# Four layers on one core: the order of every engine replaced, and each PSUM copy and residual given an engine of its own

## The chip, the cores and the metric

One Trainium2 chip, of which the program uses one core. The metric is the device time of one execution in microseconds. Of the kernel before there are three runs: 394.34, 394.36 and 395.02 us, median 394.36.

## The reference

x has 2048 rows of 512 bf16 numbers. Four layers follow one another, A, B, A, B, each `x = x + layer(layernorm(x))`, with 32 heads of 16:

```python
def _A_ref(x, wqkv, w_phi, wo):            # linear attention
    q, k, v = heads(x @ wqkv)
    pq, pk = q @ w_phi, k @ w_phi          # per head
    phi_q = concat([softmax(pq), softmax(-pq)])
    phi_k = concat([softmax(pk), softmax(-pk)])
    kv = phi_k^T @ v;  z = sum over rows of phi_k
    return (phi_q @ kv) / (phi_q @ z + 1e-6) @ wo

def _B_ref(x, wqkv, wo):                   # each row looks at rows s, s-2, ..., s-14
    q, k, v = heads(x @ wqkv)
    attn = softmax(q . k[s - 2*w] * 0.25)  # w = 0..7
    return sum_w attn * v[s - 2*w] @ wo
```

kv and z of a layer A are sums over all 2048 rows, so nothing of that layer's second half can begin before its last row has been through the first half.

## The kernel before

The rows are cut into four blocks of 512, each of four tiles of 128. L counts the two A-B pairs (0 and 1), b the blocks (0 to 3); "10" below is L = 1, b = 0. The work of a block is a chain of stages:

- `s_ln_first` and `s_norm` (L303 to L391): sums and squares of a tile (VectorE L371, ScalarE L382), variance (L309 to L313), reciprocal root on ScalarE (L317, L320), normalised tile (VectorE L325), transposes on TensorE (L338), copies of the transposed halves out of PSUM (L344): one half on ScalarE, one on VectorE.
- `s_fold` (L219) multiplies the query and key weights of layer A with w_phi once: transposes (L229), copy wT (L233), product (L238), copy WA (L242). `s_load_B` loads the weights of B and reorders them on GpSimd (L263). `s_bound` squares WA on GpSimd (L285) for a test of the range.
- `s_a1`: key and value products (L451, L463), exponentials Ek (ScalarE L457), value copies vaug (ScalarE L470), softmax sums and product (VectorE L477 to L497), then kv for all blocks in three PSUM banks (L506). `s_a2`: query products (L534), exponentials Eq (L540). `s_akv`: kv out of PSUM (VectorE L575, L582); this is the barrier of the layer, "akv0" and "akv1" below.
- `s_a3`: denominators (L603 to L622) and the product with Eq (L635, or L655 where the factor went through DRAM). `s_a4`: numerator (L680), copy oT (ScalarE L686), and in `s_out` the output product (L401), the residual (VectorE L414), squares for the next norm (ScalarE L421), and `s_norm` again.
- `s_b1`: q, k and v of layer B (L702), each copied out of PSUM by ScalarE (L716). `vrep` (L745) copies V of a block 16 times shifted within SBUF, from SP's queue: 16 DMAs of 131 KB, tiles Vg. `s_b2`: products of Q with eight shifts of K (VectorE L770), summed on TensorE (L777), exponential, softmax. `s_b3`: products with Vg (VectorE L830, "pav"), summed on TensorE (L837), copy oT (L843), then `s_out`; in the last layer `s_out` stores.

Every operation is a step, filed under a stage and an engine. `_ORDER` (L45) is a list of base-36 numbers, one for each step: it says which stage and engine gets its next step recorded. So it fixes the order on TensorE, VectorE, ScalarE and SP, each of which takes its list strictly in turn and waits by semaphore, and also the order in which buffers are handed out: 8 PSUM banks, 8 big SBUF buffers (Ek, prod, Vg, pav), 16 medium ones.

Of the kernel before, what the change touches and what calls it, by code (L numbers as in the profile page):

```python
# [8 lines left out]
BF16 = mybir.dt.bfloat16  # L9
# [7 lines left out]
P = 128  # L17
NJ = 16
D = 512
# [17 lines left out]
_OPT = {"rho_dma": ((0, 2), (0, 3), (1, 2), (1, 3)), "pe_resid": {}, "tr_dma": (), "stat_act": (), "fold_act": 0,  # L37
        "evac_act": ()}
# [7 lines left out]
1 1 0 1 0 1 i 0 i 0 i i 0 1 i 0 i 0 2 i 0 2 0 2 1 2 c 0 m n d m 3 4 m n 3 4 m 3 n 3 c n f e c g 4 c d c 4 c f  # L46
3 e 6 e 6 4 7 6 7 3 3 5 a 9 5 a 9 a 9 a 9 4 3 9 5 7 3 t u 6 d j j 5 r j 3 a 7 j 9 9 h j 9 r 9 j s 6 j s 7 j r
s 6 j r s 6 6 j s 6 k j s s j k l l k l l k l b l b b l b 8 l 9 8 8 s 8 o t a t v 7 15 u o u 15 v 16 o 16 15 6
16 o 15 16 v 16 y 16 16 y 16 z y 19 z z y 19 z 17 18 17 z 17 z z 17 z p t 12 18 10 11 o 10 u 10 11 18 v 10 12
11 w q 19 q 11 19 q v 18 q f f f h f h 12 1a x g x 12 x 19 x g 1g 13 12 1k 1g 1h 1h 1g 1h 1h 1g 1h 1h 14 1h 14  # L50
1k 14 1h 1g 14 1h 1e 1e 1f 1f 1e 1f 1f 1e 1f 1f 1b 1f 1b 1b 1f 1e 1b 1f 1n 1c 1n 1n 1n 1n 1c 1d 1n 1d 1c 1d 1d
1c 1d 1d 2c 1d 1i 1d 2d 1o 2e 1j 1c 2d 1j 2c 1d 1i 2d 1p 2c 1j 2d 1q 2d 1i 1j 1p 1i 2d 1j 1j 2d 1o 1j 2d 1j 1p
1i 1p 3r 1j 1p 1o 1p 1p 31 1p 1l 1p 1l 1p 1m 1r 1r 1m 1s 1r 1s 32 1r 1s 2d 1s 1t 2d 33 1t 1u 32 1t 1v 1u 34 1t
1u 1v 3s 2f 1v 2f 1u 2g 2f 2g 2f 34 1v 1u 34 2g 1v 2g 2h 1u 3t 1u 1t 1u 1t 2i 2h 1v 1u 1t 3s 2j 1t 2i 2h 3u 1u
2j 2h 34 2i 1y 1z 2i 1y 32 3u 2j 3u 1y 2j 2i 1y 1z 2j 1w 1z 2i 1z 2i 2h 2i 1x 2h 2i 1w 2j 2q 32 2h 2h 1x 35 2i
35 36 23 35 36 3u 35 36 2o 36 2o 23 2o 2o 3s 1w 1w 1x 3s 2k 1x 23 2k 2l 2k 2l 2k 2l 23 3v 2l 3v 3w 3v 3w 3v 3w
2m 3w 2m 2n 2s 2m 2n 2m 2n 20 21 2s 2t 2n 20 20 21 2s 2t 21 20 37 2s 21 22 21 2t 2p 22 37 2p 22 2p 22 38 37 2p
22 38 39 22 2t 38 2r 2u 37 2r 2u 3g 2r 2t 38 39 2r 3x 2u 2r 2r 3x 3y 2r 39 2s 3x 2r 39 38 2r 3x 2p 2r 3z 3y 2r
39 24 3y 2r 3z 24 2r 38 3z 24 38 2r 38 37 2r 38 37 37 2r 3y 39 37 24 22 38 22 3z 2v 22 3e 3f 22 3e 22 22 25 3e
22 3f 2v 22 25 2w 22 3f 3e 22 2x 3a 3f 2v 3f 3h 2w 3b 3h 3a 2x 3h 3h 3a 3b 2v 3h 3h 2w 3b 3h 3a 2x 3h 3h 3c 3y  # L60
3b 23 3h 3z 2w 3h 3d 3y 24 3h 3y 2x 3y 2y 3h 25 3y 3h 3i 2y 3h 3h 2y 2y 2z 3j 2z 30 3x 3x 2z 30 3x 3x 3c 2z 3z
3y 3c 30 23 30 40 2z 3d 26 40 30 41 40 3d 41 40 41 26 42 41 42 43 26 42 43 42 43 27 43 26 27 28 27 28 44 45 3i
44 28 27 45 44 28 3i 29 45 29 29 2a 29 2a 2b 2a 3j 2b 3j 2a 2b 44 2z 2b 2a 2y 45 2z 3c 2z 2b 47 2z 2y 3d 47 2a
2y 2y 2a 30 47 29 2a 29 47 2a 29 2b 3i 47 4q 4r 47 29 47 4q 47 47 4o 4r 2a 47 2z 47 3j 4p 47 46 59 3k 48 47 3k
47 4q 4p 47 5a 4q 47 5a 48 3j 4r 59 4r 3k 59 48 59 5a 5a 4o 5a 5a 4o 3i 4p 4o 4p 4p 49 4p 49 4p 48 4p 49 5a 4h
5a 59 4i 3l 4i 49 5a 4h 4a 4h 4a 3l 4i 3m 4i 49 3n 4h 4a 3l 3m 5b 3n 4i 5b 5c 48 5c 3m 3l 5c 5b 3n 5c 5b 5c 5c
4j 4k 4b 3m 4j 5c 3n 4b 3o 5c 4i 4c 4i 3o 4d 4i 4b 3o 4k 4c 3o 4d 4b 4c 5b 4d 4j 5c 3p 4c 4k 3p 4j 3q 3p 4d 4e
3q 3p 3q 4e 4f 3q 3p 4e 4g 4f 3q 4e 4f 4k 4g 3p 3p 4g 3o 3p 3o 3p 3q 3o 4f 3o 3p 4g 4v 4f 4s 4v 4g 4w 4v 4w 4f
4f 4w 4v 4f 4w 4f 4w 4s 4x 4y 4l 4x 4w 4s 4x 4l 4y 4w 4s 4x 4y 4l 4t 4e 4e 4e 4y 4e 4l 5d 4f 4w 4g 4s 5d 5e 5d
# [12 lines left out]
7w 7v 7b 7w 7b 7x 7b 6p 7w 7b 7x 7b 7w 7x 7b 7b 6q 7x 82 7b 6q 6r 7b 6q 6r 7y 7z 82 83 7y 6r 7y 7z 82 83 7z 7y
7z 82 83 81 81 81 81 7f 81 83 81 84 81 84 83 81 81 7f 7g 84 81 81 81 7h 81 81 82 7g 81 7f 81 7h 7f 7g 7h 6p 7g
7h 7i 85 6q 7i 6r 85 86 6s 85 87 86 6s 87 85 6s 86 6s 87 7j 7i 7j 86 7j 7k 7i 87 6t 6t 88 7j 6u 88 6t 7k 88 6t
89 6u 88 89 89 8a 89 8a
"""


class _Fast:

    def __init__(self, ctx, tc, A_x, A_wqkv, A_w_phi, A_wo, B_wqkv, B_wo, out):
# [14 lines left out]
        for n in ("xnT", "oT", "Eq", "rS", "kvp", "K", "QT", "Vg", "PT", "vh"):  # L106
            setattr(self, n, {})
# [18 lines left out]
    def step(self, stage, eng, fn, *args):  # L126
        key = stage + "." + eng
        if key not in self.threads:
            self.threads[key] = []
            self.names.append(key)  # L130
        self.threads[key].append(lambda: fn(*args))

# [84 lines left out]
    def s_fold(self, qk):  # L217
# [14 lines left out]
        def ev(pr, copy):  # L232
            copy(out=T["wT"][:, pr * 2:pr * 2 + 2, :].rearrange("p a b -> p (a b)"), in_=T[pr][:])  # L233

# [6 lines left out]
        def ev2(m, copy):  # L241
            copy(out=self.WA[:, m, qk * D:(qk + 1) * D], in_=T["f", m][:])  # L242

        for pr in range(2):
            add(st, "PE", tr, pr)
            add(st, *(("DVE", ev, pr, nc.vector.tensor_copy) if pr == 0 and not _OPT["fold_act"] else
                      ("ACT", ev, pr, nc.scalar.copy)))
        for m in range(NB):
            add(st, "PE", mm, m)
            add(st, *(("DVE", ev2, m, nc.vector.tensor_copy) if m % 2 == 0 and not _OPT["fold_act"] else  # L250
                      ("ACT", ev2, m, nc.scalar.copy)))
# [52 lines left out]
    def s_norm(self, st, key, b, T):  # L304
        nc, add = self.nc, self.step

        def var():
            T["q"] = self.sm([4], "q")
            nc.vector.scalar_tensor_tensor(out=T["q"][:], in0=T["sums"][:], scalar=-1.0 / D, in1=T["sums"][:],  # L309
                                           op0=ALU.mult, op1=ALU.mult)  # L310
            T["nm"] = self.sm([4], "nmean")
            nc.vector.tensor_scalar(out=T["nm"][:], in0=T["sums"][:], scalar1=-1.0 / D, scalar2=None, op0=ALU.mult)
            nc.vector.tensor_tensor(out=T["q"][:], in0=T["q"][:], in1=T["ss"][:], op=ALU.add)  # L313

        def ln():
            T["lnv"] = self.sm([4], "lnv")
            nc.scalar.activation(out=T["lnv"][:], in_=T["q"][:], func=ACT.Ln, bias=self.eps_t[:, 0:1],  # L317
                                 scale=1.0 / D)
            T["rstd"] = self.sm([4], "rstd")
            nc.scalar.activation(out=T["rstd"][:], in_=T["lnv"][:], func=ACT.Exp, scale=-0.5)  # L320

        def ap(t):
            if t == 0:
                T["xn"] = self.med([4, D], "xn")
            nc.vector.tensor_scalar(out=T["xn"][:, t, :], in0=self.x[b][:, t, :], scalar1=T["nm"][:, t:t + 1],  # L325
                                    scalar2=T["rstd"][:, t:t + 1], op0=ALU.add, op1=ALU.mult)
# [1208 lines left out]
```

## Time and profile before

| | |
|---|---|
| runs, median | 394.36 us |
| profiled execution | 393.82 us, its span 392.1 us |
| TensorE busy | 341.3 us, 87% of the span |
| VectorE busy | 321.6 us, 82% |
| ScalarE busy | 273.8 us, 70% |
| GpSimd busy | 19.9 us, 5% |
| mean granted TensorE clock | 0.965 |

The span runs from the first to the last instruction; the execution's own time is 1.72 us longer. PE is TensorE, DVE VectorE, ACT ScalarE, POOL GpSimd, SP the engine that issues most DMAs. A row of the timeline has start and length in us, engine, line, operation, tiles; in brackets the idle time before it and who ended it. A row of a group has busy us, mean ns of one, and idle before it. A row of a stretch has, for each engine, its busy time and instructions, then the granted clock, the DMA share and GB/s.

### The profile page before, as it was taken

To read this page: it belongs to the slowest core of one execution; us is meant where nothing else is said; L and a number is where in the kernel's file an instruction comes from. 1 tells how busy PE (TensorE), PEld (TensorE's weight loads), DVE (VectorE), ACT (ScalarE), POOL (GpSimd) and SP (SyncE) were. 2 spreads that over 40 slices of the span, in tenths; PEclk is the share of its full clock that TensorE was granted. 3 is DMA by queue.
4 is the path that set the end of the run, shared out by engine and by line. 5 is a ranking of instruction groups with operands and counts; after the bars stand their busy time and mean duration, and the time that the engine had idled before them with its cause. 6 is when DMAs were issued, how large, how long until landed. Compare 5 with 4: busy or idle time off the path is not lost.

```text
span 392.1 us, 7308 instructions
## 1 busy us (share of the span) xinstructions
PE 341.3 (87%) x2841; PEld 159.0 (41%) x2841; DVE 321.6 (82%) x484; ACT 273.8 (70%) x619; POOL 19.9 (5%) x40
## 2 busy tenths in 40 slices
PE   1859998989999997999999999969999978993691
PEld 1525465543444332444433457533443322331130
DVE  6684594288798886999899988599799868997993
ACT  5779986867757885768997998656977773663220
POOL 2250007200000000000000000000000000000000
PEclk9959999999999999999999999999999999997598
DMA  8920000001520599954800000044000399698404
GB/s 248 351 48 0 2 0 2 2 3 32 143 56 0 108 152 151 163 93 94 128 3 0 3 0 3 5 112 115 2 1 2 76 151 160 146 165 160 80 29 142
DMA packets 17242, 30.65 MB, mean 78 GB/s; under 512 B 4272, under 2 KB 11952, under 8 KB 17200
## 3 DMA queue, kind: packets, MB, share of 16 engines
q1 hardware_dynamic: 16672, 30.09, 38.7%
q8 instruction: 24, 0.39, 0.5%
q14 instruction: 18, 0.15, 0.1%
q10 hardware_dynamic: 528, 0.02, 0.1%
HBM read 10.50 MB, written 2.36 MB: 33 GB/s over the span
## 4 chain that ended last, share of the span: by engine, by line
PE 52%; DVE 18%; ACT 12%; DMA 10%; SPq 3%; issue 2%; POOL 0%; ACTq 0%; DVEq 0%; POOLq 0%
PE ps L702 16%; DMA Vg<-V 10%; PE ps L451 7%; PE ps L401 6%; PE ps L463 6%; PE ps L534 4%; SPq L745 3%; DVE x L414 3%; PE ps L338 3%; DVE pav L830 3%; DVE Eq L635 3%; PE ps L777 3%; PE ps L506 2%; ACT sqd L421 2%; DVE Ek L497 2%
## 5 line engine op out<-in xcount | busy, mean ns | idle before, releaser
L702 PE MATMUL ps<-xnT,WB 128*128 128x512 bf16 x384 | 89.8, 379 | 1.0 <-DVE xnT L344 0.8
L830 DVE TENSOR_TENSOR pav<-PT,Vg 128x4096 bf16<-128x4096 bf16 x32 | 71.9, 2288 | 9.5 <-DMA Vg<-V 9.4
L770 DVE TENSOR_TENSOR prod<-QT,K 128x4096 bf16<-128x4096 bf16 x32 | 71.8, 2285 | 3.8 <-ACT K L716 1.9
L702 PEld LDWEIGHTS <-WB 128*128 128x128 bf16 x384 | 35.4, 98 | 49.5 <-issue 10.5
L414 DVE SCALAR_TENSOR_TENSOR x<-ps,x 128x512 bf16<-128x512 f32 x64 | 41.1, 686 | 2.0 <-PE ps L401 1.6
L401 PEld LDWEIGHTS <-oT 128*128 128x128 bf16 x256 | 23.5, 98 | 35.6 <-issue 7.1
L540 ACT ACTIVATE Eq<-ps 128x512 bf16<-128x512 f32 x64 | 33.6, 615 | 4.9 <-PE ps L534 4.9
L421 ACT ACTIVATE sqd<-x 128x512 bf16<-128x512 bf16 x48 | 29.9, 625 | 7.9 <-DVE x L414 7.8
L843 ACT CAST oT<-ps 128x512 bf16<-128x512 f32 x32 | 18.7, 590 | 22.5 <-PE ps L837 22.5
L457 ACT ACTIVATE Ek<-ps 128x512 bf16<-128x512 f32 x64 | 33.5, 670 | 0.3 <-PE ps L451 0.3
L837 PE MATMUL ps<-pav,indAV 128*32 128x512 bf16 x256 | 20.9, 417 | 14.0 <-DVE pav L830 14.0
L338 PE MATMUL ps<-ident,xn 128*128 128x128 bf16 x256 | 20.8, 231 | 14.0 <-DVE xn L325 11.3
L401 PE MATMUL ps<-WoA,oT 128*128 128x512 bf16 x128 | 30.8, 380 | 1.4 <-ACT oT L686 1.1
L534 PE MATMUL ps<-xnT,WA 128*128 128x512 bf16 x128 | 30.1, 379 | 2.1 <-DVE WA L242 1.6
L463 PE MATMUL ps<-WA,xnT 128*128 128x512 bf16 x128 | 31.8, 397 | 0.1
L401 PE MATMUL ps<-WoB,oT 128*128 128x512 bf16 x128 | 31.2, 388 | 0.1
L451 PE MATMUL ps<-WA,xnT 128*128 128x512 bf16 x128 | 30.4, 391 | 0.5 <-ACT xnT L344 0.5
L716 ACT CAST V<-ps 128x512 bf16<-128x512 f32 x32 | 18.5, 588 | 14.9 <-PE ps L702 14.7
L325 DVE TENSOR_SCALAR xn<-x,nmean,rstd 128x512 bf16<-128x512 bf16 x64 | 23.4, 424 | 4.9 <-ACT rstd L320 4.9
L338 PEld LDWEIGHTS <-xn 128*128 128x128 bf16 x256 | 16.8, 103 | 21.8 <-DVE xn L325 16.6
L716 ACT CAST QT<-ps 128x512 bf16<-128x512 f32 x32 | 18.8, 590 | 9.4 <-PE ps L702 9.2
L716 ACT CAST K<-ps 128x512 bf16<-128x512 f32 x32 | 18.5, 585 | 9.6 <-PE ps L702 9.5
(109 smaller groups left out, 449.9 us busy)
## 6 DMA issues: line engine op xcount, KB each, us to landing
Vg<-V SPq DMA_DIRECT2D x128, 131.5 KB, 5.8
Prho<-rd SPq DMA_DIRECT2D x8, 512.0 KB, 4.7
out_dram<-x SPq DMA_DIRECT2D x8, 256.0 KB, 2.2
x<-in_A_x_dram SPq DMA_DIRECT2D x3, 512.0 KB, 8.1
wbraw<-in_B_wqkv_dram SPq DMA_DIRECT2D x3, 512.0 KB, 8.8
wraw<-in_A_wqkv_dram SPq DMA_DIRECT2D x2, 512.0 KB, 6.2
x<-in_A_x_dram SPq DMA_DIRECT2D x4, 128.0 KB, 2.4
WA<-in_A_wqkv_dram SPq DMA_DIRECT2D x1, 512.0 KB, 4.0
```

Of the source, the lines that this page charges most:

```text
L338: nc.tensor.transpose(T["pt", t // 2][:, (t % 2 * NB + c) * P:(t % 2 * NB + c + 1) * P], T["xn"][:, t, c * P:(c + 1) * P], self.ident[:])
L401: nc.tensor.matmul(y[:], lhsT=oT[:, c, t * P:(t + 1) * P], rhs=Wo()[:, c, :], start=(c == 0), stop=(c == NB - 1 and t not in pe_res))
L414: nc.vector.scalar_tensor_tensor(out=xb[:, t, :], in0=T[t][:], scalar=1.0, in1=xb[:, t, :], op0=ALU.mult, op1=ALU.add, **kw)
L421: nc.scalar.activation(out=sqd[:], in_=xb[:, t, :], func=ACT.Square, accum_out=T["ss"][:, t:t + 1])
L451: nc.tensor.matmul(pk[:], lhsT=xnT[:, t, k, :], rhs=self.WA[:, k, D:2 * D], start=(k == 0), stop=(k == NB - 1))
L463: nc.tensor.matmul(pv[:], lhsT=xnT[:, t, k, :], rhs=self.WA[:, k, 2 * D:3 * D], start=(k == 0), stop=(k == NB - 1))
L534: nc.tensor.matmul(pq[:], lhsT=self.WA[:, k, hb * P:(hb + 1) * P], rhs=xnT[:, :, k, :], start=(k == 0), stop=(k == NB - 1))
L540: nc.scalar.activation(out=self.Eq[L, b][s][:, :, hb, :], in_=T[hb][:].rearrange("p (t i) -> p t i", t=4), func=ACT.Exp, scale=1.0 - 2.0 * s)
L702: nc.tensor.matmul(pp[:], lhsT=self.WB[:, k, i, c, :], rhs=xnT[:, :, k, :], start=(k == 0), stop=(k == NB - 1))
L716: nc.scalar.copy(out=dst, in_=T[i, c][:])
L770: nc.vector.tensor_tensor(out=pr[:], in0=QT[:, c:c + 1, :].to_broadcast([P, NW, TB]), in1=win, op=ALU.mult)
L830: nc.vector.tensor_tensor(out=pv[:], in0=PT[:].unsqueeze(1).to_broadcast([P, NB, 2, TB]), in1=vw, op=ALU.mult)
```

## The change

Four things change.

1. `_ORDER` is replaced as a whole: 1423 steps instead of 1515 (the four vrep steps of a quarter are one step now).
2. Each copy out of PSUM, and each residual, is a step of its own kind (`flex`), and a string `_CHOICE` of 0 and 1 tells its engine. For a copy 1 means VectorE, 0 ScalarE. For a residual 0 means VectorE as before; 1 means that TensorE adds x with an identity matmul into the same PSUM bank and ScalarE writes the sum back. 27 of 64 residuals are so: 8 of the first A-B pair and 19 of the second.
3. The first layer norm uses BN_STATS and BN_AGGR on VectorE, without squares on ScalarE, and block 0 is normalised in two halves, tiles 2 and 3 first.
4. Memsets of a ones column, and of the first halos of K and V, become GpSimd steps that the order places.

The diff, cut to its core (two lines of the table stand for it):

```diff
-_OPT = {"rho_dma": ((0, 2), (0, 3), (1, 2), (1, 3)), "pe_resid": {}, "tr_dma": (), "stat_act": (), "fold_act": 0,
-        "evac_act": ()}
+_OPT = {"rho_dma": ((0, 2), (0, 3), (1, 2), (1, 3)), "tr_dma": ()}
...
-1 1 0 1 0 1 i 0 i 0 i i 0 1 i 0 i 0 2 i 0 2 0 2 1 2 c 0 m n d m 3 4 m n 3 4 m 3 n 3 c n f e c g 4 c d c 4 c f
...
+4 1r 4 0 5 4 0 1 4 4 6 6 0 0 2 0 2 3 n o n 7 16 16 p n q n r n n t 15 8 8 8 8 16 16 1a u u s 13 8 19 9 8 8 8 8
...
+    def flex(self, stage, fn, *args):
+        k = self.nflex
+        self.nflex += 1
+        self.step(stage, "F%d%s" % (k, fn.__name__), fn, *args, _CHOICE[k] == "1")
+
+    def copy(self, dve, out, in_):
+        if dve:
+            self.nc.vector.tensor_copy(out=out, in_=in_)
+        else:
+            self.nc.scalar.copy(out=out, in_=in_)
...
+            def stat(t):
...
+                nc.vector.bn_stats(out=T["stat"][:, t - t0, :], in_=self.x[b][:, t, :])
+                nc.vector.bn_aggr(out=T["mv"][:, t - t0, :], in_=T["stat"][:, t - t0, :])
...
+        if b == 0:
+            part((0, 1))
+            part((2, 3))
+        else:
+            part((0, 1, 2, 3))
...
+        def mm(t, onpe):
...
+            if onpe:
+                nc.tensor.matmul(y[:], lhsT=self.ident[:], rhs=xb[:, t, :], start=False, stop=True)
...
+        def res(t, onpe):
...
+            if onpe:
+                kw = {} if last else {"accum_out": T["sums"][:, t:t + 1]}
+                nc.scalar.activation(out=xb[:, t, :], in_=T[t][:], func=ACT.Identity, **kw)
...
-            add(st, "ACT", ev, t)
+            self.flex(st + "v", ev, t)
...
-        for dl in range(4):
-            for g in range(4):
-                add(st + "v", "SP", vrep, dl, g)
+        for dl in range(4):
+            add(st + "v", "SP", vrep, dl)
```

Three places in the order. The first is VectorE's start, from the mask product PHI on (x_84 is block 0 of x, x_85 block 1). Before:

```order
L212 TENSOR_TENSOR PHI<-phis,maskH 128x512
L371 TENSOR_REDUCE sums<-x_84 128x1 x4
L309 SCALAR_TENSOR_TENSOR q<-sums 128x4
L312 TENSOR_SCALAR nmean<-sums 128x4
L313 TENSOR_TENSOR q<-q,ss 128x4
L325 TENSOR_SCALAR xn<-x_84,nmean,rstd 128x512 x4
L344 COPY xnT<-ps 128x1024
L233 COPY wT<-ps 128x1024
L371 TENSOR_REDUCE sums<-x_85 128x1 x4
L233 COPY wT<-ps 128x1024
L242 CAST WA<-ps 128x512
L309 SCALAR_TENSOR_TENSOR q<-sums 128x4
```

After, from the second pair of statistics on:

```order
L379 BN_STATS stat<-x_84 128x6
L380 BN_AGGR mv<-stat 128x2
L379 BN_STATS stat<-x_84 128x6
L380 BN_AGGR mv<-stat 128x2
L384 COPY q<-mv 128x2
L379 BN_STATS stat<-x_84 128x6
L380 BN_AGGR mv<-stat 128x2
L334 TENSOR_SCALAR xn<-x_84,q,rstd 128x512 x2
L384 COPY q<-mv 128x2
L334 TENSOR_SCALAR xn<-x_84,q,rstd 128x512 x2
L146 COPY xnT<-ps 128x1024
L146 COPY wT<-ps 128x1024
```

Block 0 is normalised in two pairs of tiles; after its copies come block 1's four statistics, with one copy of the folded weights ahead of them and none behind them (the rest is ScalarE's).

The second is ScalarE in the second half of layer pair 1, where block 0's projected V leaves PSUM. Before (the last V row is block 0's fourth cast):

```order
L344 COPY xnT<-ps 128x1024
L716 CAST V<-ps 128x512 x2
L716 CAST K<-ps 128x512 x4
L317 ACTIVATE lnv<-q,eps_t 128x4
L320 ACTIVATE rstd<-lnv 128x4
L716 CAST QT<-ps 128x512
L784 ACTIVATE E,stE<-ps 128x512 x2
L716 CAST QT<-ps 128x512 x3
L716 CAST V<-ps 128x512
L798 ACTIVATE lnd<-ps,tiny_t 128x512
L800 ACTIVATE rden,stR<-lnd 128x512
L716 CAST V<-ps 128x512
```

After (L148 is the helper for copies on ScalarE; the last two V casts and the two before them are block 0's, in the order third, fourth, first, second):

```order
L148 CAST QT<-ps 128x512
L148 CAST K<-ps 128x512 x2
L148 CAST QT<-ps 128x512
L148 CAST V<-ps 128x512
L148 CAST oT<-ps 128x512 x2
L148 CAST V<-ps 128x512
L148 CAST K<-ps 128x512
L148 CAST oT<-ps 128x512
L148 COPY xnT<-ps 128x1024 x2
L148 CAST K<-ps 128x512
L148 CAST V<-ps 128x512 x2
```

Before, block 1's K and Q stand between block 0's V casts; now block 0's V is mostly among its own Q and K, with one K of block 1 ahead of the last two casts. On TensorE the fourth V projection of block 0 is the eleventh projection after the barrier now; it was the twentieth, with the output products and transposes of three other blocks among them. Its first two V casts stand on ScalarE behind block 1's transposed halves (xnT) and first K cast.

The third is VectorE's end. Before:

```order
L830 TENSOR_TENSOR pav<-PT,Vg 128x4096 x7
L414 SCALAR_TENSOR_TENSOR x_86<-ps,x_86 128x512 x3
L414 SCALAR_TENSOR_TENSOR x_85<-ps,x_85 128x512 x2
L414 SCALAR_TENSOR_TENSOR x_86<-ps,x_86 128x512
L414 SCALAR_TENSOR_TENSOR x_85<-ps,x_85 128x512 x2
L414 SCALAR_TENSOR_TENSOR x_87<-ps,x_87 128x512 x4
L864 TENSOR_REDUCE tot<-ps 128x1
```

After:

```order
L843 TENSOR_TENSOR PT<-E,rden 128x1024
L868 TENSOR_TENSOR pav<-PT,Vg 128x4096 x6
L421 SCALAR_TENSOR_TENSOR x_84<-ps,x_84 128x512
L421 SCALAR_TENSOR_TENSOR x_86<-ps,x_86 128x512
L421 SCALAR_TENSOR_TENSOR x_84<-ps,x_84 128x512
L421 SCALAR_TENSOR_TENSOR x_86<-ps,x_86 128x512 x3
L902 TENSOR_REDUCE tot<-ps 128x1
```

Twelve residuals behind the last product have become six; those of blocks 1 and 3 and half of block 0's are ScalarE's. The last products are block 2's and no longer block 3's.

308 lines of the change are left out of this document (158 added, 150 removed).

## The prediction

> **What bounds the kernel now.** I read the page's totals and clock row first, then the busy time of each engine by stage, then the timeline of the first 28 us, the chain of waits over the end, and the groups by line for durations.
>
> ```profile
> span 392.1 us, 7308 instructions
> PE 341.3 (87%) x2841; PEld 159.0 (41%) x2841; DVE 321.6 (82%) x484; ACT 273.8 (70%) x619; POOL 19.9 (5%) x40
> PEclk9959999999999999999999999999999999997598
> core 0: us, PE busy (x) PEld busy (x) DVE busy (x) ACT busy (x) POOL busy (x), PEclk, DMA share, GB/s
> 0.00:27.00 27.00, 13.04 (x97) 8.41 (x98) 20.46 (x53) 17.43 (x44) 9.56 (x30) 0.86 0.77 235
> 8.00:27.00 19.00, 13.04 (x97) 8.41 (x98) 14.77 (x31) 13.08 (x33) 7.15 (x16) 0.81 0.78 239
> 27.00:73.00 46.00, 43.73 (x386) 25.45 (x385) 25.32 (x37) 39.27 (x82) 9.10 (x2) 0.97 0.00 1
> 73.00:249.00 176.00, 168.72 (x1441) 78.73 (x1439) 152.43 (x230) 138.62 (x317) 0.98 (x6) 1.00 0.37 63
> 249.00:386.00 137.00, 115.84 (x927) 46.45 (x924) 123.18 (x164) 78.48 (x176) 0.30 (x2) 0.95 0.49 92
> 386.00:392.10 6.10, 0.00 (x0) 0.00 (x0) 0.21 (x2) 0.00 (x0) 0.00 (x0) 0.69 0.26 85
> ```
>
> I cut at 73 and 249 us because there the key-value sums of a whole layer (akv0, akv1) become ready and nothing of that layer's second half can go ahead of them. The three stages have different limits. Stage 2 is TensorE's: 168.7 of 176 us busy, so 7.3 us are idle. Stage 3 is not: TensorE has 115.8 of 137, VectorE 123.2, so VectorE is the fullest and has 13.8 us idle. Stage 1 wastes its start: between 8 and 27 us TensorE is busy 13.0 of 19 us, at a mean clock of 0.81.
>
> ```profile
> 4.08 2.46 DVE L371 TENSOR_REDUCE sums<-x 128x1 f32<-128x512 bf16 x4
> 7.61 1.38 DVE L325 TENSOR_SCALAR xn<-x,nmean,rstd 128x512 bf16<-128x512 bf16 x4 [0.60 <-ACT rstd L320]
> 8.08 1.89 PE L338 MATMUL ps<-ident,xn 128*128 128x128 bf16 x16 [8.08 <-DVE xn L325]
> 21.11 1.22 PE L338 MATMUL ps<-ident,xn 128*128 128x128 bf16 x8 [2.80 <-DVE xn L325]
> 24.82 0.61 PE L338 MATMUL ps<-ident,xn 128*128 128x128 bf16 x4 [2.48 <-DVE q L309]
> 27.35 8.32 PE L451 MATMUL ps<-WA,xnT 128*128 128x512 bf16 x32
> ```
>
> TensorE starts at 8.08 and stands twice, 2.80 and 2.48 us, for the normalised block 1; dense work begins at 27.35. In stage 3 the chain of waits hangs on the V copies: block 0's projected V is complete late, and from there the copies Vg<-V follow each other to the end.
>
> ```profile
> 274.06 1.03 PE ps L702 x4
> 307.97 0.59 ACT L716 CAST V<-ps 128x512 bf16<-128x512 f32 x1
> 339.88 0.56 ACT L716 CAST V<-ps 128x512 bf16<-128x512 f32 x1
> 340.47 23.42 SPq L745 DMA_DIRECT2D Vg<-V  x32
> 363.31 5.49 DMA Vg<-V
> 369.92 8.89 DVE pav L830 x4
> 378.81 7.18 DVE x L414 x12
> 386.10 0.15 DVE L866 TENSOR_SCALAR fl<-tot 128x1 int32<-128x1 f32 x1
> ```
>
> Block 0's V is whole at 308.56, 59.6 us into stage 3 and 34.5 after its first projection (274.06). Blocks 2 and 3 go out as 32 issues from 340.47, the last landing at 368.80: 28.3 us for two blocks. Then four products (8.89) and twelve residuals in a row on VectorE (7.18, 0.60 each), then 6 us of end.
>
> **The change, part by part.** Durations:
>
> ```profile
> 110.69 8.63 PE ps L702 x40
> 66.00 0.56 PE ps L548 x32
> L371 DVE TENSOR_REDUCE sums<-x 128x1 f32<-128x512 bf16 x16 | 9.9, 674 | 0.0
> L312 DVE TENSOR_SCALAR nmean<-sums 128x4 f32<-128x4 f32 x16 | 2.6, 162 | 0.0
> L344 DVE COPY xnT<-ps 128x1024 bf16<-128x1024 bf16 x16 | 10.9, 687 | 7.0 <-PE ps L338 6.9
> L242 DVE CAST WA<-ps 128x512 bf16<-128x512 f32 x4 | 2.7, 686 | 0.3 <-PE ps L238 0.3
> L716 ACT CAST QT<-ps 128x512 bf16<-128x512 f32 x32 | 18.8, 590 | 9.4 <-PE ps L702 9.2
> L611 DVE TENSOR_TENSOR DR<-ps,rS 128x256 f32<-128x256 f32 x8 | 3.4, 422 | 2.8 <-PE ps L603 2.7
> L784 ACT ACTIVATE E<-ps 128x512 bf16<-128x512 f32 x16 | 9.5, 599 | 2.5 <-PE ps L777 2.5
> L784 ACT ACTIVATION_READ_ACCUMULATOR E<-ps 128x1 f32 x16 | 3.3, 206 | 0.0
> ```
>
> A 512-column product costs TensorE 0.216 us (8.63/40), a projection of four 0.86.
>
> *Residuals.* 27 of 64 go to ScalarE: 8 in stage 2, 19 in stage 3. Each takes 0.60 us from VectorE and adds one identity product (0.216) on TensorE. The ScalarE operation is not in the trace; from PSUM with an accumulator it lies between the plain cast, 0.59, and E with its read, 0.81; I take 0.7 because 17 of the 27 accumulate. Stage 3: VectorE -11.4, TensorE +4.1, ScalarE +13.3. ScalarE has 58 us free there and TensorE 21, so this is hidden; if it were not, TensorE's 4.1 would be lost. Stage 2: VectorE -4.8, TensorE +1.7, and TensorE is the bound: that part counts.
>
> *Copies.* Of the vaug, K, Q, V and oT casts, all on ScalarE before, VectorE takes 21, at 0.69 against 0.59; the transposed blocks go the other way, from 16 on VectorE to 11, and four WA casts and one wT copy leave it. By stages, VectorE: stage 2, -4 transposes (-2.8), +10 casts (+6.9), one DR more (+0.4 and its sum): no net change beside the residuals' -4.8. Stage 3: -3 transposes (-2.1), +4 casts (+2.8), one DR less (-0.7). So VectorE's stage 3 falls by 11.4, to 111.8.
>
> *First normalisation.* Sixteen ScalarE squares go, and sixteen reduces become BN_STATS and BN_AGGR, neither of which the trace has. Nearest for the first is the reduce, paced 0.6 (2.46/4), and for the second the 0.16 of nmean. Four pairs end at 4.08 + 4 x 0.76 = 7.1, and the first normalised tile starts near 7.3 where it now starts at 7.61, since the first half's rstd is computed meanwhile. Bounds: an aggregation wholly overlapped gives 6.5; a two-pass BN_STATS (2 x 0.67 + 0.16) gives 10.1. I take 7.3, no change worth counting: the start of TensorE stays at 8.
>
> *Order in stage 1.* The fold of the key weights moves ahead of half of block 0's V, block 0's key products follow at once, and block 1's statistics no longer stand behind two copies and wait for ScalarE squares. The two waits (2.80, 2.48) lose their cause. Of 6.0 us idle between 8 and 27 I leave 2, because block 1's normalisation still needs x and VectorE in turn: -4.0. The clock of 0.81 over 19 us cost at most 3.6; with denser work I take back half, -1.8. Four query projections move in and two sums (0.56 each) move out: +2.3. Stage 1: 73 - 3.5 = 69.5. In "TensorE: Matmul & The Clock Gate" (What's actually happening) the Trainium skill says that the clock is halved until about 3.4 us of activity and after as long an idle window. By that rule gaps under 3.4 us cost no clock, and all 3.6 would come back, 1.8 less than my sum; the trace does not bear it out: the third digit of PEclk (19.6 to 29.4 us) is 5, where no gap is above 2.80.
>
> *Order in stage 2.* The same four projections leave (-3.5), one sum comes (+0.6), identities +1.7: -1.2. Of 7.3 idle I take half back, since all three engines are nearly full there and each in-order queue has to wait for the others somewhere. 176 - 1.2 - 3.6 = 171.2.
>
> *Order in stage 3.* V of block 0 is projected after eleven projections, 9.5 us after the first. Two of its casts stand behind block 1's first K, which has 6.5 us of TensorE work ahead of it (five groups of four, three pairs, sixteen transposes); with the casts 17 us after the first projection, not 34.5. So its copies start some 17 us earlier, and the copies stop being the chain. Its place is taken by VectorE: 111.8 us of work. For idle I keep 13.8: the waits for Vg go, but the last residuals now wait, one by one, for a copy and four projections (8 products 0.5, cast 0.59, four groups 3.5, residual 0.6: about 5.5 against 7.18 now). 125.6. On SP, blocks 2 and 3 now interleave, half of block 2 behind all of block 3; VectorE uses them in that order. On GpSimd the ones column of the last block of the second layer is now written between two weight copies, so one of the 16 medium buffers is held until stage 2; that costs nothing unless buffers run out, which no row of now shows, and I give it no price.
>
> Sum: 69.5 + 171.2 + 125.6 + 6.1 (end unchanged) = 372.4 us of span. The profiled execution took 393.82 for 392.1, 1.7 more: 374.1; the runs' median (394.36) is 0.5 above that execution. Forecast 375.
>
> **The rivals.**
>
> ```profile
> L285 POOL TENSOR_TENSOR sq<-WA x2: 3594/4567/5540, 61.5 to 67.0; 128x2048 bf16<-128x2048 bf16 x2
> 61.28 2.29 DVE L497 TENSOR_TENSOR Ek<-Ek,rk 128x4096 bf16<-128x4096 bf16 x1
> 20.36 1.31 DVE L325 TENSOR_SCALAR xn<-x,nmean,rstd 128x512 bf16<-128x512 bf16 x2
> 25.01 0.41 DVE L325 TENSOR_SCALAR xn<-x,nmean,rstd 128x512 bf16<-128x512 bf16 x1
> ```
>
> *GpSimd blocks VectorE* (0.12). The two squares of WA now run while VectorE had only one product to do; one took 5.54 us beside that product, which kept its 2.29, the other 3.59 alone. Normalising took 0.7 each where GpSimd copied weights (20.36) and 0.41 alone (25.01). So the two do hinder each other, and the later starter loses. In the new order query weights fold earlier, and the squares fall among VectorE's sums and products: up to 2 x 3.59 = 7.2 on VectorE before the first barrier. 375 + 7 = 382. "SBUF — State Buffer" (SBUF: two separate sides) in the Trainium skill says the same more strictly: whoever starts first holds the shared ports for its whole instruction; the rows agree.
>
> *The waits only move* (0.15). Stages 1 and 2 keep their idle, and only VectorE's shorter stage 3 counts: 375 + 5.8 + 3.6 = 384. For it: three engines at 79 to 96% in stage 2. Against it: the two early waits have a plain cause that goes.
>
> *Better packed than I allow* (0.12). All idle of stage 2 goes (-3.6) and half of stage 3's (-6.9): 364.5.
>
> *Block 2's V comes too late* (0.09; slower). On TensorE its fourth projection now stands behind block 1's first sum of products, which waits for block 1's copies. From block 2's last V cast to the end: 28.3 for two blocks' copies, 4.4 for two products, 6 for the tail, 6.1 and 1.7: 46.5. It replaces VectorE as the bound once that cast ends after 328 (328 + 28.3 + 4.4 = 361, where VectorE's last product ends by my sum: 240.7 + 125.6 - 5.5), and gives a slower kernel after 348.7; it ends at 340.44 now. Ten us beyond now, 350.5, gives 397. Against it: the projections ahead of it amount to about 71 us of TensorE from the second barrier, so with 10 idle I expect it near 322.
>
> *The order changes and the chain does not* (0.04): 394.
>
> **How the numbers follow.** Forecast 0.48, its own range 370 to 380. Faster: 0.48 + 0.12 + 0.15 + 0.12 = 0.87; same 0.04; slower 0.09. (0.2%, 0.8 us, is what a measurement of this kernel can tell.) The range takes in 364.5, both middle rivals and a two-pass BN_STATS (+3): 364 to 389.
>
> **What would show it.** Right: dense TensorE work before 20 us; second barrier near 241 instead of 249; block 0's V whole about 42 us after it instead of 59.6; VectorE without waits for Vg; residuals on ScalarE near 0.7 us. Wrong: VectorE idle in stage 3 above 20 us; Vg among its releasers again; a products' group of the first stage stretched beside GpSimd.

## The result, and the profile after

The changed kernel takes 368.44 us (median of 4 runs, 368.0 to 369.3), the kernel before beside it 394.35: a ratio of 0.9351, 95% interval 0.9318 to 0.9385. The forecast was 375.0, from 364 to 389. The profiled execution took 368.67 us for a span of 367.0.

First the page's totals and clock row of the changed kernel, to be laid beside those of before.

```profile
span 367.0 us, 7333 instructions
PE 336.5 (92%) x2868; PEld 162.5 (44%) x2868; DVE 318.5 (87%) x460; ACT 272.9 (74%) x622; POOL 18.8 (5%) x40
PEclk9999999999999999999999999999999999999897
```

The busy sums of the three engines hardly moved: VectorE 321.6 to 318.5, ScalarE 273.8 to 272.9, TensorE 341.3 to 336.5. So nearly all of the 25 us of span are waiting that went, not work that went (TensorE's 4.8 is the largest share of work). The 5 in the third digit of the clock row is gone. The stretches by stage say where (they end where the first akv0 and akv1 products start on VectorE, at 66.7 and 234.7 us, and at the flag `fl`, VectorE's last result).

```profile
0.00:66.70 66.70, 56.46 (x431) 33.69 (x432) 53.82 (x103) 47.34 (x96) 15.62 (x34) 1.00 0.31 94
8.00:27.00 19.00, 18.25 (x138) 11.35 (x139) 14.29 (x35) 12.20 (x25) 7.19 (x15) 1.00 0.77 237
66.70:234.70 168.00, 164.04 (x1467) 79.28 (x1465) 151.85 (x220) 137.22 (x321) 3.18 (x7) 1.00 0.37 67
234.70:360.60 125.90, 116.00 (x977) 49.49 (x974) 112.79 (x138) 88.38 (x205) 0.00 (x0) 0.99 0.50 99
360.60:367.00 6.40, 0.00 (x0) 0.00 (x0) 0.00 (x0) 0.00 (x0) 0.00 (x0) 0.62 0.32 106
```

| stage | before | forecast | after |
|---|---|---|---|
| 1, to akv0 | 73.0 | 69.5 | 66.7 |
| 2, to akv1 | 176.0 | 171.2 | 168.0 |
| 3, to the flag | 137.0 | 125.6 | 125.9 |
| end | 6.1 | 6.1 | 6.4 |

Between 8 and 27 us TensorE is now busy 18.25 of 19 us at a clock of 1.00 (before 13.04 at 0.81). In stage 3 VectorE still is the fullest, with 112.8 of 125.9 us. The rows of the timeline that answer to those of before, and two on GpSimd:

```profile
7.75 0.70 DVE L334 TENSOR_SCALAR xn<-x,q,rstd 128x512 bf16<-128x512 bf16 x2
8.19 1.96 PE L348 MATMUL ps<-ident,xn 128*128 128x128 bf16 x16 [8.19 <-DVE xn L334]
11.65 3.05 PE L481 MATMUL ps<-WA,xnT 128*128 128x512 bf16 x8
...
37.52 4.15 POOL L300 TENSOR_TENSOR sq<-WA 128x2048 bf16<-128x2048 bf16 x1 [12.65 <-ACT WA L148]
38.25 3.97 DVE L505 TENSOR_TENSOR s<-s 128x1024 bf16<-128x1024 bf16 x1
...
276.41 3.62 PE L727 MATMUL ps<-xnT,WB 128*128 128x512 bf16 x16
277.95 1.08 ACT L148 CAST V<-ps 128x512 bf16<-128x512 f32 x2
279.06 59.73 SPq L779 DMA_DIRECT2D Vg<-V  x64
292.05 8.90 DVE L868 TENSOR_TENSOR pav<-PT,Vg 128x4096 bf16<-128x4096 bf16 x4
314.85 0.61 ACT L148 CAST V<-ps 128x512 bf16<-128x512 f32 x1
333.46 0.17 DVE L893 TENSOR_SCALAR_CACHE_REDUCE junk<-stE 128x16 f32<-128x16 f32 x1 [2.68 <-ACT E L822]
340.79 13.30 DVE L868 TENSOR_TENSOR pav<-PT,Vg 128x4096 bf16<-128x4096 bf16 x6
```

Block 0's V is whole at 279.03, 44.3 us after the second barrier (59.6 before), and its transfers start at once. Block 2's last V cast, on which the slower rival hung, ends at 315.46 (340.44 before). Among the groups, the products (pav) wait 0.3 us in all, none of it named as Vg (the first row is before), and the new residual on ScalarE has a price:

```profile
L830 DVE TENSOR_TENSOR pav<-PT,Vg 128x4096 bf16<-128x4096 bf16 x32 | 71.9, 2288 | 9.5 <-DMA Vg<-V 9.4
...
L868 DVE TENSOR_TENSOR pav<-PT,Vg 128x4096 bf16<-128x4096 bf16 x32 | 71.4, 2288 | 0.3
L418 ACT ACTIVATE x<-ps 128x512 bf16<-128x512 f32 x27 | 15.8, 598 | 7.6 <-PE ps L411 7.4
L148 ACT COPY xnT<-ps 128x1024 bf16<-128x1024 bf16 x21 | 21.1, 1035 | 3.3 <-PE ps L348 3.3
```

### The profile page after: what moved, and what is told of

The parts are those of the page before. It is cut to its first block, busy times and chain, and to the rows that moved or that the text cites. A ratio compares the mean times of both kernels' runs of the same rounds, so it can differ in the third digit from the quotient of the medians.

```text
span 367.0 us, 7333 instructions
## 1 busy us (share of the span) xinstructions
PE 336.5 (92%) x2868; PEld 162.5 (44%) x2868; DVE 318.5 (87%) x460; ACT 272.9 (74%) x622; POOL 18.8 (5%) x40
## 4 chain that ended last, share of the span: by engine, by line
PE 64%; DVE 16%; ACT 9%; DMA 6%; issue 2%; SPq 1%; DVEq 0%; ACTq 0%
PE ps L727 23%; PE ps L408 13%; PE ps L815 4%; PE ps L481 4%; PE ps L348 4%; PE ps L875 3%; ACT Ek L475 3%; DMA Vg<-V 3%; PE ps L705 3%; PE ps L469 3%; DVE Ek L521 2%; ACT Eq L565 2%; DVE pav L868 2%; PE ps L530 2%; DVE Eq L660 2%
## 5 line engine op out<-in xcount | busy, mean ns | idle before, releaser
L727 PE MATMUL ps<-xnT,WB 128*128 128x512 bf16 x384 | 88.0, 379 | 0.0
L148 ACT CAST oT<-ps 128x512 bf16<-128x512 f32 x58 | 33.1, 602 | 17.6 <-PE ps L875 11.5
L408 PE MATMUL ps<-WoB,oT 128*128 128x512 bf16 x128 | 32.7, 390 | 0.0
L421 DVE SCALAR_TENSOR_TENSOR x<-ps,x 128x512 bf16<-128x512 f32 x37 | 24.4, 685 | 5.8 <-PE ps L408 5.7
L348 PE MATMUL ps<-ident,xn 128*128 128x128 bf16 x256 | 19.7, 225 | 8.4 <-DVE xn L334 8.4
L875 PE MATMUL ps<-pav,indAV 128*32 128x512 bf16 x256 | 18.9, 391 | 7.0 <-DVE pav L868 5.2
L148 ACT COPY xnT<-ps 128x1024 bf16<-128x1024 bf16 x21 | 21.1, 1035 | 3.3 <-PE ps L348 3.3
L521 DVE TENSOR_TENSOR Ek<-Ek,rk 128x4096 bf16<-128x4096 bf16 x8 | 18.3, 2289 | 5.5 <-ACT rk L518 5.5
L148 ACT CAST QT<-ps 128x512 bf16<-128x512 f32 x30 | 17.5, 586 | 5.6 <-PE ps L727 5.3
L418 ACT ACTIVATE x<-ps 128x512 bf16<-128x512 f32 x27 | 15.8, 598 | 7.6 <-PE ps L411 7.4
```

What stands on the lines that cost most here:

```text
L148: self.nc.scalar.copy(out=out, in_=in_)
L348: nc.tensor.transpose(U["pt", t // 2][:, (t % 2 * NB + c) * P:(t % 2 * NB + c + 1) * P], self.xn[key, b][:, t, c * P:(c + 1) * P], self.id ...
L408: nc.tensor.matmul(y[:], lhsT=oT[:, c, t * P:(t + 1) * P], rhs=Wo()[:, c, :], start=(c == 0), stop=(c == NB - 1 and not onpe))
L727: nc.tensor.matmul(pp[:], lhsT=self.WB[:, k, i, c, :], rhs=xnT[:, :, k, :], start=(k == 0), stop=(k == NB - 1))
```

## The experiments

The change has two halves, an order of the steps and an engine for each copy and residual. The theory after the result was that both count by themselves: the order takes waits away, the residuals take work off VectorE, and the copies' engines matter little. The rivals were that one half is the whole. All kernels compute the same; unless said otherwise they are the changed kernel with one edit.

**All residuals back on VectorE.** The 27 ones of the residuals become zeros, as in the last line of `_CHOICE`:

```diff
-    "0000001100001000000000000000000000001111000100010000000000000000000000000011110000000000000000001111"
+    "0000000000001000000000000000000000000000000100000000000000000000000000000000000000000000000000000000"
```

> The changed kernel with all 27 residuals of TensorE and ScalarE put back on VectorE; the order of the steps is as after. Theory (stage 2 is bound by TensorE, stage 3 by VectorE's work, so that the 19 residuals of stage 3 are what made stage 3 shorter): VectorE gets 19 x 0.685 = 13.0 us more in stage 3 and 8 x 0.685 = 5.5 us more in stage 2, where TensorE loses 8 x 0.379 = 3.0 us; stage 3 grows from 125.9 by 6 to 13 us, stage 2 changes by -3 to +5.5, the whole is 375 to 387 us. Rival (the order alone made the gain, and VectorE's 13.3 us of idle time in stage 3 takes the residuals in): 366 to 370 us, stage 3 near 126.

Measured: 387.22 us (ratio to before 0.9816, 0.9778 to 0.9853), 18.8 more than the changed kernel and at the upper end of the theory. The rows are stages 2 and 3.

```profile
64.90:242.20 177.30, 165.67 (x1460) 78.86 (x1458) 156.65 (x236) 132.62 (x305) 3.26 (x7) 0.99 0.34 63
242.20:377.50 135.30, 116.28 (x958) 48.38 (x955) 124.01 (x165) 77.77 (x177) 0.00 (x0) 0.95 0.48 93
```

Stage 3 is 9.4 us longer, for 11.2 us more of VectorE's work: as the theory had it. Stage 2 is 9.3 us longer, outside its -3 to +5.5: eight residuals of 0.685 us cost 1.2 us each. TensorE has eight products less to issue there and is idle 11.6 us, where it was 4.0. So stage 2 is not bound by TensorE's work alone; VectorE's, at 156.7 of 177.3 us, counts too. The order was kept, so this is what the residuals are worth in the new order, not by themselves.

**Copies back.** 47 of the 300 choices turned to the old engine, shown by the first of the three lines:

```diff
-    "1011101101000000000000010100011110100100100000000011000000000001101001000010001000000010000000111000"
+    "0101010110101010101000000000000000000000100001000000000000000001100100000010010000000000000000111001"
```

> The changed kernel with every PSUM copy on the engine that it had before (47 of 300 choices turned back); residuals and order as after. Theory (copies set only which engine a step waits for; in stage 2 six more copies net go to ScalarE, which works 137 of 168 us): 368 to 374 us. Rival (the copies' engines are what keeps TensorE fed in stages 1 and 2): stage 1 back at 70 us or more and stage 2 at 172 or more, the whole 378 us or more.

Measured: 409.34 us (1.0355, 1.0312 to 1.0397), 40.9 more than the changed kernel and slower than before. The theory fell here, and all three signs of the rival came (72.2 us for stage 1, 193.6 for stage 2). Stages 2 and 3:

```profile
72.20:265.80 193.60, 170.65 (x1469) 80.50 (x1466) 148.63 (x215) 139.42 (x327) 3.21 (x7) 0.96 0.33 58
265.80:402.00 136.20, 119.57 (x976) 50.08 (x973) 112.02 (x137) 87.85 (x206) 0.00 (x0) 0.96 0.48 93
```

Stage 2 is 25.6 us longer though VectorE has 3.2 us less work than after and ScalarE 2.2 more. What a copy costs is not its duration but who waits for it. A part of it is slower matmuls: TensorE has the same products in stage 2 and is busy 6.6 us longer, at a granted clock of 0.96 instead of 1.00.

**The order alone, and the engines alone.** The first kernel has the new order, all residuals on VectorE and all copies on their old engines (both edits above). The second has the order of before, written in the names of the changed kernel, with the changed engines and the new statistics; its first block is normalised whole:

```diff
-        if b == 0:
-            part((0, 1))
-            part((2, 3))
-        else:
-            part((0, 1, 2, 3))
+        part((0, 1, 2, 3))
```

> The changed kernel's order with every copy and every residual on the engine that it had before: the order, the first block's halves and the new statistics alone. Theory (order and engines both count; stage 3 loses what the residuals gave): 376 to 389 us, stage 1 near 67, stage 3 from 132 to 139. Rival A (the order is all): 367 to 372 us. Rival B (an order made for other engines is worth nothing without them): 392 us or more.

> The order of before, on the changed kernel's code: its engines for copies and residuals and its new statistics, but the first block normalised whole. Theory (in the old order stage 3 waits for block 0's V and its transfers, 59.6 us after the second barrier, so work taken off VectorE turns into waiting there; the head keeps its idle TensorE): 384 to 394 us, stage 1 near 72. Rival (the engines' choice makes the gain): 370 to 380 us.

Measured: the order alone 425.92 us (1.0795, 1.0745 to 1.0845), the engines alone 415.19 (1.0504, 1.0452 to 1.0556). Both are slower than before. For the first only its rival B had that; the second lies outside its theory and its rival. Stage 3 of the second:

```profile
264.10:408.00 143.90, 120.77 (x946) 48.37 (x943) 113.59 (x138) 89.30 (x203) 0.30 (x2) 0.95 0.49 89
```

VectorE has 113.6 us of work there, 9.6 less than before, and the stage is 6.9 longer: work was taken off VectorE and became waiting, as the theory said. But the theory's reason, block 0's V, is only a part of it. Of VectorE's 30.3 us idle there 7.1 ended with a transfer of V, against 5.7 of 13.8 before; the other waits are spread over several causes:

```profile
DVE pav L864 <- DMA Vg<-V: 7.1, 4, 2.9
DVE q L436 <- ACT sqd L424: 4.8, 3, 2.4
DVE tot L898 <- PE ps L896: 3.7, 1, 3.7
```

(A row of waits has who waited for whom, us in total, times, the longest.) To have a clean corner for the comparison, a third kernel has the order and the engines of before with the new statistics alone.

> The order and the engines of before, with the new statistics alone (one statistics and one aggregation instruction on VectorE, 0.84 us a tile, in place of a sum on VectorE of 0.67 us and a square on ScalarE), the first block whole. Theory (VectorE gets 16 x 0.17 = 2.7 us more and ScalarE 16 x 0.8 = 13 us less in stage 1, where TensorE's idle time and low clock cost more than either): 391 to 396 us. Rival (the 13 us of ScalarE are what shortened stage 1): 388 us or less.

Measured: 397.47 us (1.008, 1.0049 to 1.011), 3 us slower than before, a little beyond the theory. Its profiled execution is 5.0 us longer in span, and only 1.2 of that lie in stage 1 (74.2 us), where the new statistics are; what lengthened stages 2 and 3 by 1.9 and 2.0 was not looked for. TensorE's two early waits are still there:

```profile
21.83 1.22 PE L348 MATMUL ps<-ident,xn 128*128 128x128 bf16 x8 [2.63 <-DVE xn L334]
25.94 0.61 PE L348 MATMUL ps<-ident,xn 128*128 128x128 bf16 x4 [2.89 <-DVE xn L334]
```

They are there too with the engines alone (1.94 and 3.60 us), and with the new order and the old engines no wait of TensorE between 9 and 28 us is above 0.84. So they belonged to the order.

From this corner the order adds 28.5 us, the engines 17.7; if they added, they would come to 46 and make 443.6. They make 368.44. **The two halves do not add: 75 us lie in their fitting each other.**

**Which copies.** 19 of the 47 are copies of transposed blocks (xnT), 28 are casts of projections, sums and folded weights. Each group alone went back (the first of the three lines each time):

```diff
-    "1011101101000000000000010100011110100100100000000011000000000001101001000010001000000010000000111000"
+    "0101010101000000000000010100011110100100100001000011000000000001100101000010011000000010000000111001"
```

> The changed kernel with only the 19 copies of transposed blocks (xnT) on the engine that they had before; the other 28 of the 47 changed copies stay as after. All 47 together cost 41 us. Theory (a copy of xnT releases all projections of its half block, so that TensorE stands behind it; on VectorE it sits behind products of 2.29 us): these 19 make most of it, 390 to 409 us. Rival (the loss is spread over the copies by number, 19 of 47): 380 to 390 us. Rival B (it is the 28 casts from projections that matter): 368 to 376 us.

```diff
-    "1011101101000000000000010100011110100100100000000011000000000001101001000010001000000010000000111000"
+    "1011101110101010101000000000000000000000100000000000000000000001101000000010000000000000000000111000"
```

> The changed kernel with the 28 other changed copies (casts of vaug, oT, Q, K, V and of the folded weights) on the engine that they had before; the 19 copies of xnT stay as after. All 47 back cost 41 us, the 19 of xnT alone 32 us. Theory (the costs add, since each group delays TensorE at places of its own): 41 - 32 = 9 us, 374 to 381 us. Rival (each group alone costs much, because any misplaced copy opens the same wait): 390 us or more. Rival B (the casts are harmless alone): 367 to 371 us.

Measured: the 19 alone 400.3 us (1.0184, 1.0147 to 1.0221), 31.9 more than after; the 28 alone 383.58 (0.9735, 0.9682 to 0.9788), 15.1 more. The sum is 47 where both at once cost 40.9: the casts cost somewhat more than was expected, and the two groups seem to share a few waits. How one misplaced copy costs is seen in the third stage of the kernel with the 19 (timeline of VectorE, then TensorE):

```profile
297.62 2.29 DVE L808 TENSOR_TENSOR prod<-QT,K 128x4096 bf16<-128x4096 bf16 x1
299.83 0.68 DVE L421 SCALAR_TENSOR_TENSOR x<-ps,x 128x512 bf16<-128x512 f32 x1
...
301.66 0.69 DVE L146 COPY xnT<-ps 128x1024 bf16<-128x1024 bf16 x1
302.26 0.17 DVE L753 COPY K<-K 128x64 bf16<-128x64 bf16 x1
307.58 4.49 DVE L808 TENSOR_TENSOR prod<-QT,K 128x4096 bf16<-128x4096 bf16 x2 [5.15 <-ACT QT L148]
...
293.19 1.06 PE L348 MATMUL ps<-ident,xn 128*128 128x128 bf16 x16
302.49 5.30 PE L727 MATMUL ps<-xnT,WB 128*128 128x512 bf16 x16 [4.36 <-DVE K L753]
```

The transposes are done at 294.25. The copy stands in VectorE's row behind three products, a cast and three residuals and starts at 301.66, 7.4 us later. TensorE's next projections read it; TensorE stands 4.36 us and then runs 16 projections in 5.30 us, which in the changed kernel take 3.62. (The row names the K halo, a copy of 0.17 us that follows; the projections read xnT.) The longer run is a lower clock: TensorE's granted clock was 0.54 in the first 2.5 us after the wait, 0.80 in the next 2.8, and 1.00 from there on to 311.0.

```profile
302.49:305.00 2.51, 2.51 (x7) 1.00 (x8) 0.00 (x0) 0.77 (x2) 0.00 (x0) 0.54 0.00 0
305.00:307.80 2.80, 2.80 (x12) 1.09 (x10) 0.21 (x1) 2.00 (x5) 0.00 (x0) 0.80 0.18 72
```

Their Q is what VectorE's next products need, and so VectorE stands 5.15 us in its turn. One copy of 0.69 us, two engines standing.

**The same 19, placed early.** If the place in the row is the cost, it can be mended without changing the engine: the 12 copies that go to VectorE stand directly behind their transposes in the order. The one told of above moves so on VectorE:

```diff
+L146 COPY xnT<-ps 128x1024
 L808 TENSOR_TENSOR prod<-QT,K 128x4096 x2
 L146 CAST QT<-ps 128x512
 L808 TENSOR_TENSOR prod<-QT,K 128x4096
 L421 SCALAR_TENSOR_TENSOR x_86,sums<-ps,x_86 128x512 x3
-L146 COPY xnT<-ps 128x1024
 L753 COPY K<-K 128x4x16
```

> The kernel with the 19 copies of xnT on their old engines, which took 400.3 us, but the 12 of them that go to VectorE stand in the order directly behind their transposes (8 of the 12 had 2 to 7 steps of VectorE ahead of them there, up to four products of 2.29 us). Theory (the copy's place in VectorE's row is what costs, not the engine): most of the 32 us comes back, 375 to 388 us. Rival A (VectorE lacks the time or waits for the transposes instead, so the place does not help): 395 to 405 us.

Measured: 398.0 us (1.0105, 1.0039 to 1.0171): 2.3 us better, not 12 to 25, and the intervals of the two kernels overlap. The theory fell. VectorE's waits for transposes, first with the copies late and then early, show one thing that took the place:

```profile
DVE xnT L146 <- PE ps L348: 7.1, 7, 2.1
...
DVE xnT L146 <- PE ps L348: 14.2, 12, 3.0
```

Placed late, the copies make TensorE wait: 13.0 us in all for VectorE's xnT (the 4.36 above among them). Placed early, they cost TensorE 1.4, but VectorE stands 7.1 us more, 14.2 in 12 waits, for transposes that TensorE has not done yet. The other seven of the 19 went to ScalarE and kept their places; TensorE waits 5.9 us for ScalarE's xnT in both kernels, so what better places for these seven would give stays open. On ScalarE, which has 31 and 37 us free in stages 2 and 3 of the changed kernel, 21 such copies waited 3.3 us in all for transposes in the changed kernel, and TensorE did not wait for any of them. A new order of the whole for the old engines might find better places; that was not tried.

**Block 0's V late.** Its four projections, casts and first transfers move behind that block's denominators in the last layer, in the order of steps only; on ScalarE:

```diff
-L148 CAST V<-ps 128x512
 L148 CAST oT<-ps 128x512 x2
-L148 CAST V<-ps 128x512
...
-L148 CAST V<-ps 128x512 x2
...
-L148 CAST V<-ps 128x512 x2
+L148 CAST V<-ps 128x512 x6
```

> The changed kernel with the four V projections of block 0 in the second B layer, their casts and first transfers moved behind the denominators of that block, so that block 0's V is whole some 15 us later (near 294 instead of 279 us), with all engines as after. Theory (the transfers of Vg take 60 us in one row and VectorE's first pav comes 13 us after their start; VectorE then waits for Vg as before, up to 10 us, and has no other step to take in the meantime): pav waits 7 to 12 us for Vg, and the whole is 375 to 380 us. Rival (VectorE is behind anyway, the delay is taken in): 367 to 371 us.

Measured: 383.53 us (0.9749, 0.9711 to 0.9786), 15.1 more than after.

```profile
294.64 58.40 SPq L779 DMA_DIRECT2D Vg<-V  x64
300.18 2.29 DVE L868 TENSOR_TENSOR pav<-PT,Vg 128x4096 bf16<-128x4096 bf16 x1 [10.89 <-DMA Vg<-V]
```

The transfers start at 294.64, about 15 us later than in the changed kernel and 61.6 after the second barrier (59.6 before), and VectorE stands 10.9 us for the first and 3.6 for the next: 14.5 in all. The direction held; the size was beyond the theory, which had left out the later waits, since the products (2.29 us) run faster than the four transfers of about 0.9 us that each needs (58.40/64). Nothing took the delay in. This prices an early V in the new order; in before, with V as late, VectorE stood only 5.7 us for Vg in this stage, so the 15.1 are not what the earlier V gained there.

**Head and ports.** Three small parts. First the halves: the edit shown above by itself, with one logarithm and exponent for block 0.

> The changed kernel with its first block normalised whole: four statistics, one logarithm and exponent, four tiles, as in the other blocks. All else as after. Theory (the first normalised tile waits for two more statistics of 0.84 us and the pair on ScalarE no longer runs beside them): TensorE starts about 1.0 us later, near 9.2 us, and as TensorE is busy nearly throughout stage 1 the whole is 0.7 to 1.5 us longer, 369 to 370. Rival (the halves are hidden by the transfer of the weights or by TensorE's slow start): 368 to 368.7 us.

Measured: 368.41 us (0.9367, 0.9338 to 0.9395), the rival: the halves give nothing that can be told. TensorE starts at 8.62 us there, 0.4 later than after and not 1.0; other kernels with the changed order start between 8.0 and 8.5. Then GpSimd's first square, given to VectorE where it stands idle:

```diff
-            nc.gpsimd.tensor_tensor(out=T[qk][:], in0=w, in1=w, op=ALU.mult)
+            (nc.gpsimd if qk else nc.vector).tensor_tensor(out=T[qk][:], in0=w, in1=w, op=ALU.mult)
...
-            add("bound", "POOL", sq, qk)
+            add("bound", "POOL" if qk else "DVE", sq, qk)
```

> The changed kernel with the first of GpSimd's two squares of the folded weights (sq 0) given to VectorE, placed just before the akv0 products, where VectorE sits idle 4.15 us. Theory (GpSimd's 4.15 us square held VectorE's add of line 505 for 3.3 us, 0.69 to 3.97 us, and TensorE then waited 1.29 us for the next cast of vaug; TensorE is otherwise busy from 27 us on): line 505 has no instance over 1 us, and the time falls by about 1.3 us, 366.5 to 367.5. Rival A (VectorE's lost time counts in full): 365 us. Rival B (the lost time lies beside TensorE's work, nothing changes, or the square on VectorE delays the barrier): 368 to 370 us.

Measured: 367.27 us (0.9315, 0.9286 to 0.9344). The eight adds of line 505 (shortest, median, longest, in ns) are all alike now:

```profile
L505 DVE TENSOR_TENSOR s<-s x8: 685/692/693, 32.9 to 224.3; 128x1024 bf16<-128x1024 bf16 x8
```

So the square was what held the add. That it gains 1.2 us is what the theory asked for, but the intervals of the two kernels overlap. Last, with that edit, one product of block 1 moved into VectorE's wait of 2.68 us:

```diff
-L868 TENSOR_TENSOR pav<-PT,Vg 128x4096 x2
+L868 TENSOR_TENSOR pav<-PT,Vg 128x4096
 L753 COPY K<-K 128x4x16
 L808 TENSOR_TENSOR prod<-QT,K 128x4096 x8
+L868 TENSOR_TENSOR pav<-PT,Vg 128x4096
 L893 TENSOR_SCALAR junk,okc<-stE 128x16
```

> The changed kernel with two moves: the first square on VectorE ahead of the akv0 products (367.3 us by itself), and the last pav of block 1 in the last layer behind the products of blocks 2 and 3, with its matmuls and cast and the first output matmul of that block behind it. Theory (VectorE waits 2.68 and 1.12 us for the last softmax because it has no other step left; one pav of 2.29 us fills the first gap, and the products come 2.29 us earlier): 364.5 to 366.5 us. Rival (block 1's transferred V keeps its buffer 18 us longer, and the transfers of blocks 2 and 3 or a product wait for it): 367.5 us or more.

Measured: 365.63 us (0.928, 0.9237 to 0.9323), the fastest kernel of the study; against the changed kernel about 0.8% less, where the intervals just touch.

```profile
310.88 0.18 DVE L753 COPY K<-K 128x64 bf16<-128x64 bf16 x1 [2.14 <-ACT K L148]
329.30 2.29 DVE L868 TENSOR_TENSOR pav<-PT,Vg 128x4096 bf16<-128x4096 bf16 x1
331.50 0.17 DVE L893 TENSOR_SCALAR_CACHE_REDUCE junk<-stE 128x16 f32<-128x16 f32 x1
```

The gap at line 893 is filled, but the products that came earlier now wait 2.14 us for K. The third stage of the profiled execution is 126.8 us, 0.4 shorter than with the square alone (127.2) and 0.9 longer than after: most of the wait was moved, not removed. Its shorter time is a first stage of 62.8 us, where the kernel with the square alone, with the same first stage, has 64.8. Of these 2.0 us 0.4 are TensorE's earlier start (8.01 for 8.46) and 1.0 its first eight V projections (1.97 us for 2.94). So the gain is measured, but it was not shown that the filled gap made it.

## Why the prediction was right, and where not

Forecast 375.0, measured 368.44: the direction and the range hold, and the gain was 26 where 19 was expected.

- *Stage 3* came out as summed, 125.9 for 125.6, with VectorE's work at 112.8 (111.8) and its idle time at 13.1 (13.8). Both reasons were tested in the new order. With the residuals back it takes 9.4 us more (the sum had 11.4); with V late the whole takes 15.1 more. In the old order less work on VectorE made the stage longer (143.9). That the idle time came out is partly luck: the waits for Vg (5.7 us before) went as forecast, but the last residuals, which should take their place, wait 2.4 us, and most of the rest are waits that the sum did not name (2.7 and 1.1 for the last softmax, 1.7 for K, 1.5 and 1.3).
- *ScalarE's residual* was put at 0.7 us: 0.598 and, for 17 of 27, 0.2 for the read of the accumulator.
- *Stage 1* was 2.8 us better than the sum. Of the idle time 0.75 us was left, where 2 was allowed, and no clock below 1.00 is on record from 8 to 27 us, where half of 3.6 us was given back. By the Trainium skill's rule ("TensorE: Matmul & The Clock Gate", What's actually happening) all of it comes back: here the rule came nearer than the sum. The result does not test the rule, though, since the gaps went too (0.34 us is the longest named), and the first eight V projections still ran slowly at a recorded clock of 1.00 (last section). That TensorE's start would not move held (8.19 for 8.08). That the new statistics cost nothing held nearly: the old kernel with them alone takes 3 us more, but its first stage only 1.2.
- *Stage 2* is the step that failed, although its total (168.0 for 171.2) hides it. The sum charged the eight residuals there with +1.7 for TensorE's identity products, because "TensorE is the bound". With them back on VectorE the stage takes 9.3 us more: in the new order they are a gain of 9.3, not a cost of 1.7. Half of the idle time went as guessed (7.3 to 4.0); TensorE's busy time fell by 4.7 where 1.2 was summed, and since its ends are modelled the runs do not settle what of that was hidden waiting.
- *Copies* were costed by their durations and came out at "no net change". Turned back they cost 40.9 us. A sum of durations can't see what a copy is worth; the forecast was saved because it took the idle time of each stage as a whole and never priced the copies by themselves. The half of stage 2's idle time that it took back was a guess with no row behind it, and that it came near is luck.
- *The rivals.* GpSimd did block VectorE, once, for 3.3 us (0.69 to 3.97) and not twice for 3.59; the second square began while VectorE stood idle. The row agrees with the Trainium skill, "SBUF — State Buffer" (SBUF: two separate sides), that whoever starts first keeps the ports to its end. The waits did not only move, and block 2's V was whole at 315.5, before the 322 expected and the 328 from which it decides. The better-packed case (364.5) was nearer to the result than its chance of 0.12 suggests.

## What to carry to other kernels

An order of steps for in-order engines is written for one assignment of engines, and an assignment for one order: here each half without the other cost 18 to 29 us, and both together gained 26 to 29, so they have to be searched together and judged together. A small copy that releases a row of matmuls belonged here on the engine with free time, not on the one with the long instructions; its cost is the wait of the engine behind it (4.4 and 5.2 us on two engines for one copy of 0.69). Before a gap is filled, ask what must come earlier for that: in the last experiment the wait only moved to the next operand.

## What the runs showed of the hardware

- *TensorE's start differs between profiled executions with the same first instructions, and the granted clock does not show it.* The first eight V projections took 3.05 us in the profiled execution of the changed kernel and 1.89 in that of the kernel with the residuals back, whose first stage has the same instructions in the same order; 8 at 0.216 us are 1.73 and the last one's end. The clock of that stretch reads 1.00 in both.

```profile
8.29 1.97 PE L348 MATMUL ps<-ident,xn 128*128 128x128 bf16 x16 [8.29 <-DVE xn L334]
11.43 1.89 PE L481 MATMUL ps<-WA,xnT 128*128 128x512 bf16 x8
```

The Trainium skill ("TensorE: Matmul & The Clock Gate", What's actually happening) has the start at half rate for about 3.4 us of activity. The kernel with the residuals back agrees, with 3.1 us (8.29 to 11.43); the changed kernel took up to 6.3 (8.19 to 14.5), which is more than the half a microsecond of spread that this section gives.

The first stage of these kernels lies between 64.9 and 66.7 us (the changed kernel, the residuals back, V late). Differences of 2 us in stage 1 of single profiles should not be read as an edit's.
- *A long wait of TensorE is paid twice.* After standing 4.36 us it ran 16 projections in 5.30 us instead of 3.62, at a granted clock of 0.54 and then 0.80.
- *A GpSimd product under way holds up a VectorE add.* The add of two SBUF operands, 0.69 us, took 3.97 when it started 0.73 us into a GpSimd product of 4.15, and ended 0.55 after it; with that product moved to VectorE all eight adds took 0.69.
